# A recurrent attention, two expert layers and one core: the attention's small products laid out anew

## The chip, the cores and the metric

The program runs on one core of a Trainium2 chip, as one launch. The metric is device time in microseconds (us); lower is better. The engines are named as in the profile: PE (TensorE, matrix products), PEld (its weight loads), DVE (VectorE), ACT (ScalarE), POOL (GpSimd), SP (SyncE, which here only issues DMAs).

## The reference, cut to what matters

```python
def _attn_ref(r, k, v, w, a, b):          # batch 4, heads 8, 768 steps, head width 40
    state = np.zeros((B, H, D, D))
    for t in range(S):
        y[:, :, t] = np.einsum('bhd,bhde->bhe', rt, state)
        Sa = np.einsum('bhde,bhe->bhd', state, at)
        state_decay = state * wt[:, :, None, :] - np.einsum('bhd,bhe->bhde', Sa, bt)
        state = state_decay + np.einsum('bhd,bhe->bhde', vt, kt)
    return y

def reference(...):
    x = attention output as (3072 tokens, 320)
    x = moe(x)       # skip test, 8 experts, top 1: x + gate * relu(x @ w1[e]) @ w2[e], hidden 1024
    return ffn(x)    # h = x @ w_in (320 to 2048); (h * sigmoid(1.702 h)) @ w_out
```

Everything is fp32. The attention is a recurrence over 768 steps with a 40 by 40 state for each of 32 pairs of batch and head; the expert layer and the last layer are dense products over 3072 tokens.

## The kernel before, in words

**Attention.** The 768 steps are cut into 12 chunks of 64, and each chunk is solved with matrix products in fp32. Of the 128 partitions a half (64) belongs to one half of the batch (called hb, 0 or 1), and within a half there are two batch elements (par, 0 or 1) and 8 heads (h). One chunk does this:

- `g_load`, `g_prep`: the decays w are loaded and multiplied up by two scans on DVE (tile W; L212 and L225, with three small operations, L215 to L221, between them). One buffer `wt` holds the load, so the next chunk's w is loaded only when the scan has read it.
- `g_a`, `g_kb`: POOL scales a, k and b by W (tiles at, kbT). PE transposes k and b to km (L286), W to F (L247).
- `g_gram`, for a pair of chunks: PE forms the 32x32 diagonal blocks of the product of a and b (L312), ACT copies them to Za, DVE transposes them to Z (L322), and 62 DVE operations on tile tm (L336 and L339 in turn, 31 times) invert the unit triangular blocks. DVE transposes the result to Tc (L345), and DMAs put it in tz (L354), of which one chunk's chain reads.
- `g_ag` forms the full 64x64 product and masks it to tile m (L373, L378), `g_ab` forms the off-diagonal block again into tile bz (L401, L406).
- `g_chain`, once for each hb: X = m v + a S (L443, L450); then a block solve, x = -X, U = tz x, y = U, X += bz y, x = -X, U += tz x (L464 three times), with a copy on ACT between two products. tz and bz are 128 rows high, with zeros where the other batch element lies. The last U goes into vu.
- `g_state`: the next state from the old one and from k times vu (L508, L512), scaled on DVE (L516). `g_sn` transposes it (L536).
- `g_vt`, `g_pq`, `g_post`: transposes of vu (L558), products with r (L577), a mask on DVE (L579), and the output (L600, L605, L611).
- `put` and `logits` send the output to memory and form the expert logits (L837, L847); `g_route` assigns experts.
- `g_warm` puts products whose result nobody reads (L630) into PE's order.

An fp32 product is two records in the trace, an fp32 transpose one; a run of 32 products reads x64.

**Experts and last layer.** `Moe1` gathers the tokens of an expert, multiplies hi and lo fp16 parts (L1114, L1117), and again for the second product (L1153 to L1155). `Moe2` does the same with L1363, L1366 and L1403 to L1405. In L1117 and L1366 the third of three products has 64 rows of weights, the others 128.

**Order.** Nothing is a loop on the chip. Each step is a generator that yields what it waits for and what it will cost on which engine; `weave` runs through all generators and issues next what can start soonest by those costs, with the table RANK to break near ties. What comes out is one fixed order of instructions for each engine. PE, DVE, ACT, POOL and SP's DMA issue each work through their order, and wait in it.

## Time and profile before

| | |
|---|---|
| median of 3 runs | 1093.49 us (1087.88 to 1104.85) |
| profiled execution, its own time | 1083.23 us |
| profiled execution, span from first to last instruction | 1081.4 us |
| mean granted TensorE clock | 0.912 of full speed |
| PE busy | 954.4 us, 88% of the span |
| DVE, ACT, POOL busy | 588.2, 392.9, 373.1 us |

The span is read in stages: to about 117 us no chain has begun; from 117 to 536 us the chunks run; then the routing of the last tokens and the first gather; from 570 us the experts; from 727 us the last layer. [...]

### The profile page before, as it was taken

Reading aid. Unit: us, or ns where it says so; the run is one execution under the profiler, and the core shown is the slowest. Engines: PE = TensorE matmul, PEld = TensorE weight load, DVE = VectorE, ACT = ScalarE, POOL = GpSimd, SP = SyncE. Lnnn points to the kernel's source line nnn. Section 1 sums busy time; section 2 is a strip of 40 time slices with the busy share of each in tenths; the row PEclk is TensorE's granted clock in tenths of the full one; section 3 lists DMA queues with packets and bytes.
Section 4 is the critical chain, followed back from the end, with each engine's and each line's share of the span. In section 5 each row is a group of like instructions: output and inputs, shape, how many; then the busy total and the mean of one; then the engine's idle time right before and its main releaser. Section 6 shows DMA issues by size and latency. Waiting matters only on the chain.

```text
span 1081.4 us, 30855 instructions
## 1 busy us (share of the span) xinstructions
PE 954.4 (88%) x13709; PEld 706.2 (65%) x13709; DVE 588.2 (54%) x1070; ACT 392.9 (36%) x780; POOL 373.1 (34%) x277
## 2 busy tenths in 40 slices
PE   4677799999999999999607997959899999999998
PEld 4577689889888898989605774633455545555555
DVE  3589872795784954544998774579921121212110
ACT  0121234434334334234444653425433243333330
POOL 4673021333434321222234444325433243233320
PEclk8798599999999998699558997979999999999999
DMA  4332223434333232031688654442201010100000
GB/s 139 100 94 54 54 84 88 127 104 111 79 99 98 82 104 61 18 101 57 217 220 251 167 148 145 151 99 84 64 13 38 19 31 13 31 20 7 19 13 27
DMA packets 81586, 92.77 MB, mean 86 GB/s; under 512 B 58516, under 2 KB 68504, under 8 KB 77464
## 3 DMA queue, kind: packets, MB, share of 16 engines
q1 hardware_dynamic: 79144, 86.38, 28.0%
q0 software_dynamic: 2304, 4.36, 1.6%
q8 instruction: 109, 1.79, 0.7%
q14 instruction: 29, 0.24, 0.1%
HBM read 66.04 MB, written 14.48 MB: 74 GB/s over the span
## 4 chain that ended last, share of the span: by engine, by line
PE 59%; DVE 15%; DMA 10%; issue 7%; POOL 5%; ACT 2%; SPq 1%; POOLq 0%; DVEq 0%; ACTq 0%
PE g L1363 5%; PE c L1403 5%; PE c L1404 5%; PE c L1405 5%; PE g L464 4%; PE g L577 4%; PE g L1366 4%; DMA wt<-wt 3%; DMA w2s<-w 3%; PE gx L1363 3%; PE gx L464 2%; PE g L600 2%; PE g L605 2%; PE gx L443 2%; PE gx L450 2%
## 5 line engine op out<-in xcount | busy, mean ns | idle before, releaser
L1386 POOL TENSOR_TENSOR glo<-g,ghi 128x512 f16<-128x512 f32 x96 | 115.1, 1199 | 216.0 <-ACT ghi L1385 215.9
L1382 DVE SCALAR_TENSOR_TENSOR g<-g,sg 128x512 f32<-128x512 f32 x64 | 44.1, 690 | 144.8 <-ACT sg L1380 144.8
L1403 PE MATMUL c<-wo_hi,ghi 128*128 128x320 f16 x384 | 115.8, 302 | 2.6 <-ACT wo_hi L1308 2.6
L1404 PE MATMUL c<-wo_lo,ghi 128*128 128x320 f16 x384 | 115.1, 300 | 0.9 <-DVE wo_lo L1311 0.9
L1405 PE MATMUL c<-wo_hi,glo 128*128 128x320 f16 x384 | 115.2, 300 | 0.0
L1363 PE MATMUL g<-xt,wi_hi 128*128 128x512 f16 x320 | 81.8, 387 | 12.2 <-DMA xt<-xe 12.2
L1385 ACT CAST ghi<-g 128x512 f16<-128x512 f32 x96 | 59.3, 617 | 85.1 <-DVE g L1382 85.1
L1363 PEld LDWEIGHTS <-wi_hi 128*128 128x128 f16 x480 | 45.6, 99 | 59.0 <-DMA xt<-xe 12.5
L275 POOL TENSOR_TENSOR kbT<-kbT,W 128x1024 f32<-128x1024 f32 x24 | 64.3, 2689 | 40.7 <-DMA kbT<-kbT 22.5
L336 DVE TENSOR_TENSOR tmp<-tm,Z 128x252 f32<-128x252 f32 (+22 forms) x186 | 64.5, 347 | 10.3 <-PE tm L328 5.6
L1366 PEld LDWEIGHTS <-wi_lo 128*128 128x128 f16 (+1 forms) x288 | 27.9, 97 | 64.4 <-issue 42.2
L339 DVE TENSOR_TENSOR tm<-tm,tmp 128x252 f32<-128x252 f32 (+22 forms) x186 | 66.1, 355 | 5.1
L1380 ACT ACTIVATE sg<-g 128x512 f32<-128x512 f32 x64 | 38.0, 595 | 71.2 <-PE g L1366 71.2
L1382 DVE SCALAR_TENSOR_TENSOR g<-gx,sg 128x512 f32<-128x512 f32 x32 | 22.1, 689 | 76.3 <-ACT sg L1380 76.3
L464 PE MATMUL g<-x,tz 128*64 128x40 f32 x1536 | 58.2, 243 | 1.5 <-issue 1.3
L1366 PE MATMUL g<-xt,wi_lo 128*128 128x512 f16 (+1 forms) x192 | 59.2, 385 | 0.0
L1049 POOL TENSOR_TENSOR w2l<-w2s,w2h 128x1280 f16<-128x1280 f32 x16 | 42.7, 2671 | 47.5 <-ACT w2h L1047 46.6
L917 POOL DMA_INDIRECT tab<-c_pair,r_si x24 | 27.8, 1158 | 89.9 <-DVE c_pair L914 51.8
L464 PEld LDWEIGHTS g<-x,tz 128*64 128x64 f32 x1536 | 54.5, 153 | 4.2 <-issue 2.6
L261 POOL TENSOR_TENSOR at<-at,W 128x1024 f32<-128x1024 f32 x12 | 37.2, 3097 | 57.1 <-DMA at<-at 56.8
L1403 PEld LDWEIGHTS <-ghi 128*128 128x128 f16 x384 | 37.5, 98 | 28.4 <-issue 16.1
L630 PE MATMUL gx<-c 128*128 128x192 f16 x506 | 52.5, 258 | 3.8 <-DMA c<-c 3.7
(169 smaller groups left out, 2088.1 us busy)
## 6 DMA issues: line engine op xcount, KB each, us to landing
w2s<-w SPq DMA_DIRECT2D x8, 1280.0 KB
w1s<-w1a SPq DMA_DIRECT2D x8, 1024.0 KB
wt<-wt SPq DMA_DIRECT2D x24, 320.0 KB
vu<-rv SPq DMA_DIRECT2D x12, 640.0 KB
kbT<-kbT SPq DMA_DIRECT2D x24, 320.0 KB
d_s<-wo SPq DMA_DIRECT2D x10, 512.0 KB
d_s<-wia SPq DMA_DIRECT2D x8, 512.0 KB
rT<-rT SPq DMA_DIRECT2D x24, 160.0 KB
```

The costliest lines, as they stand in the source:

```text
L275: nc.gpsimd.tensor_tensor(out=t, in0=t, in1=w, op=ALU.mult)
L336: nc.vector.tensor_tensor(out=tv, in0=Tm[:, :, r0:, st:st + 1].to_broadcast([128, 2, n, st]), in1=Z4[:, :, st:st + 1, 0:st].to_broadcast([ ...
L339: nc.vector.tensor_tensor(out=Tm[:, :, r0:, 0:st], in0=Tm[:, :, r0:, 0:st], in1=tv, op=ALU.subtract)
L464: mm(z[o, d], lhsT=w[:, par, hb * 8 + h], rhs=t[:, h], start=start and h == 0, stop=True, **kw)
L1363: nc.tensor.matmul(h, lhsT=self.whi[:, k % 3, fs], rhs=xt[:, k], start=k == 0, stop=False)
L1366: nc.tensor.matmul(h, lhsT=self.wlo[:p, k, fs], rhs=xt[:p, k], start=False, stop=k == 2)
L1382: nc.vector.scalar_tensor_tensor(out=g, in0=h, scalar=2.0 ** -6, in1=sg2, op0=ALU.mult, op1=ALU.mult)
L1385: nc.scalar.copy(out=ghi[:, f], in_=g)
L1386: nc.gpsimd.tensor_tensor(out=glo[:, f], in0=g, in1=ghi[:, f], op=ALU.subtract)
L1403: nc.tensor.matmul(o, lhsT=ghi[:, f, s], rhs=self.ohi[:, f], start=f == 0, stop=False)
L1404: nc.tensor.matmul(o, lhsT=ghi[:, f, s], rhs=self.olo[:, f], start=False, stop=False)
L1405: nc.tensor.matmul(o, lhsT=glo[:, f, s], rhs=self.ohi[:, f], start=False, stop=f == 15)
```

## The change

- `g_chain` does both halves of the batch at once. Every product of X, U and the state has 64 rows and 64 columns of weights, in one of four places of the array: rows of one half, columns of one half, with the places changing from product to product. Moved columns are 48 or 64 where they were 40 (paddings are zeroed or not read).
- `g_ab` and bz are gone: `g_ag` is called for each par and forms, with a mask of two kinds (c_two), both the block that v needs and the off-diagonal block.
- `g_vt` transposes only the part of vu that is U, in halves of 64 rows; v's part comes from memory with rT. `g_pq` is 64 products of 40 rows and 64 columns in four places (uT and rT) in place of 16 of 80 rows and 128 columns. `g_post` has its second product (L582) in four places too.
- `g_gram`: the blocks of both chunks of a pair and of both batch elements lie on 128 partitions (tm is 32 by 32 on each), so Z and Tc are one transpose for a pair instead of two; the number of DVE operations stays at 62.
- `g_burst` adds 18 products that nobody reads to each of two places of each chunk, `g_warm` issues three of 128 columns where it issued two of 192, by another rule.
- Experts and last layer: the 64-row product is made a 128-row one (weights doubled). For it w1b is loaded twice from memory, and one more DMA copies lo weights of the last layer; a copy of w1h by DMA is gone.
- `weave` counts costs otherwise, many costs are other numbers, and RANK is another table, so that the order of all engines is another.

The diff, cut to its core:

```diff
--- before.py
+++ after.py
...
+                yield 'A.37'
+                nc.scalar.copy(out=Za[:, i, hb], in_=Ad[hb][:, :256])
+                self.give(sg[hb])
+        yield ('elim', c0 - 2)
+        Z = self.tile([128, 32, 32], F32, 'Z')
+        yield 'D1.95'
+        nc.vector.transpose(out=Z.rearrange('p t s -> p (t s)'), in_=Za.rearrange('p i b (g t) -> p t (i b g)', t=32))
...
         for st in range(31, 0, -1):
-            r0 = st // 2
-            n = 16 - r0
-            tv = tmp[:, :2 * n * st].rearrange('p (q a b) -> p q a b', q=2, b=st)
-            d = f'D{.06 + 2 * n * st / 960}'
+            n = 32 - st
+            tv = tmp[:, :n * st].rearrange('p (a b) -> p a b', b=st)
+            d = f'D{.17 + .00107 * n * st}'
             yield d
-            nc.vector.tensor_tensor(out=tv, in0=Tm[:, :, r0:, st:st + 1].to_broadcast([128, 2, n, st]),
-                                    in1=Z4[:, :, st:st + 1, 0:st].to_broadcast([128, 2, n, st]), op=ALU.mult)
+            nc.vector.tensor_tensor(out=tv, in0=Tm[:, st:, st:st + 1].to_broadcast([128, n, st]),
+                                    in1=Z[:, st:st + 1, 0:st].to_broadcast([128, n, st]), op=ALU.mult)
             yield d
-            nc.vector.tensor_tensor(out=Tm[:, :, r0:, 0:st], in0=Tm[:, :, r0:, 0:st], in1=tv, op=ALU.subtract)
+            nc.vector.tensor_tensor(out=Tm[:, st:, 0:st], in0=Tm[:, st:, 0:st], in1=tv, op=ALU.subtract)
         self.mark('elim', c0)
         yield ('te', c0 - 3)
         Tc = self.tile([128, 2, 512], F32, 'Tc', 2)
-        for i in range(2):
-            yield 'D1.0'
-            nc.vector.transpose(out=Tc[:, i].rearrange('p (g t d) -> p t d g', t=16, d=2), in_=Tm[:, i].rearrange('p a b -> p (a b)'))
+        yield 'D1.95'
+        nc.vector.transpose(out=Tc.rearrange('p i (u r) -> p r (i u)', r=32), in_=Tm.rearrange('p a b -> p (a b)'))
...
-                nc.sync.dma_start(out=tz[sl, 1 - q // 2, :, q % 2 * 32:q % 2 * 32 + 32], in_=Tc[sl, i].rearrange('p (u t) -> p u t', t=32))
+                nc.sync.dma_start(out=tz[sl, :, q % 2 * 32:q % 2 * 32 + 32], in_=Tc[sl, i].rearrange('p (u t) -> p u t', t=32))
...
-    def g_ag(self, c):
+    def g_ag(self, c, par):
...
         for h in range(8):
-            for par in range(2):
-                R = slice(64 * par, 64 * par + 64)
+            for q in range(2):
                 for hb in range(2):
                     r = slice(64 * hb, 64 * hb + 64)
-                    nc.tensor.matmul(ps[hb][R, 64 * h:64 * h + 64], lhsT=kbT[r, h, par, R], rhs=at[r, h, par], start=True, stop=True)
-        self.mark('ag', c)
+                    o = slice(64 * (q ^ hb), 64 * (q ^ hb) + 64)
+                    nc.tensor.matmul(ps[hb][o, 64 * h:64 * h + 64], lhsT=kbT[r, h, par, o], rhs=at[r, h, par], start=True, stop=True)
+        self.once('ag', c)
...
-    def g_ab(self, c):
...
-            for h in range(8):
-                for par in range(2):
-                    o = 64 - 64 * par
-                    nc.tensor.matmul(ps[o:o + 32, 32 * h:32 * h + 32], lhsT=kbT[r, h, par, o:o + 32], rhs=at[r, h, par, 32:],
-                                     start=True, stop=True)
...
+        self.once('gram', c)
...
-    def g_chain(self, c, hb):
-
-        nc = self.nc
-        yield (f'gram{hb}', c)
+    def g_chain(self, c):
...
+        every = [(h, par, hb, slice(48 * h, 48 * h + 48), slice(64 * par, 64 * par + 64), slice(64 * hb, 64 * hb + 64), slice(64 - 64 * hb, 128 - 64 * hb))
+                 for h in range(8) for par in range(2) for hb in range(2)]
+        yield 'P1.05*.40'
+        X = [self.pst(f'gx{hb}') for hb in range(2)]
+        self.X = X[1]
+        for h, par, hb, d, o, v, u in every:
+            mm(X[hb][o, d], lhsT=m[par][v, hb, h], rhs=vu[v, 16 * hb + 8 * par + h, :48], start=h == 0, stop=False, **kw)
...
+        for h, par, hb, d, o, v, u in every:
+            mm(X[hb][o, d], lhsT=at[v, h, par], rhs=ST[v, 8 * par + h, :48], start=False, stop=True, **kw)
...
-        times(U, self.tz, x)
-        self.once('U', c)
-        vu5 = vu.rearrange('p (b q h) x -> p b q h x', b=2, q=2)
+        x, y = self.x, self.y
+        x4, y4 = (z[:, :640].rearrange('p (b h d) -> p b h d', b=2, d=40) for z in (x, y))
+        v3 = lambda z, w: z[:, :8 * w].rearrange('p (h d) -> p h d', d=w)[:, :, :40]
+        for i in range(2):
+            for hb in range(2):
+                yield 'A.44'
+                nc.scalar.activation(out=x4[:, hb], in_=v3(X[hb], 48), func=AF.Copy, scale=-1.0)
+            if i:
+                self.mark('D', c)
+            yield '+g2'
+            sg = self.got
+            yield 'P1.05*.54'
+            U = [self.pst(z) for z in sg]
+            for h, par, hb, d, o, v, u in every:
+                mm(U[par][u, 64 * h:64 * h + 64], lhsT=tz[o, 8 * hb + h], rhs=x[o, 320 * hb + 40 * h:320 * hb + 40 * h + 64], start=h == 0, stop=True, **kw)
+            if i:
+                break
+            for par in range(2):
+                yield 'A.44'
+                nc.scalar.copy(out=y4[:, par], in_=v3(U[par], 64))
+                self.give(sg[par])
+            yield 'P1.05*.40'
+            for h, par, hb, d, o, v, u in every:
+                mm(X[hb][o, d], lhsT=m[par][u, hb, h], rhs=y[u, 320 * par + 40 * h:320 * par + 40 * h + 48], start=False, stop=True, **kw)
+            self.mark('B', c)
+        self.mark('U', c)
         for par in range(2):
-            R = slice(64 - 64 * par, 128 - 64 * par)
-            yield 'A.33'
-            nc.scalar.copy(out=vu5[R, hb, par], in_=v3(U)[R])
-        self.give(sc)
-        self.once('vu', c)
+            for hb in range(2):
+                yield 'A.42'
+                u = slice(64 - 64 * hb, 128 - 64 * hb)
+                o = 16 * hb + 8 * par
+                nc.scalar.copy(out=vu[u, o:o + 8, :40], in_=v3(U[par], 64)[u])
+            self.give(sg[par])
+        self.mark('vu', c)
...
-                    mm(ps[64 * hb:64 * hb + 40, 40 * h:40 * h + 40], lhsT=km[:, p], rhs=vu[:, p], start=False, stop=True, **kw)
+                    mm(ps[64 * hb:64 * hb + 40, 64 * h:64 * h + 64], lhsT=km[:, p], rhs=vu[:, p], start=False, stop=True, **kw)
...
-            ps = self.pst(sg)[:80]
-            for j in range(4):
-                o = 320 * q + 80 * j
-                nc.tensor.transpose(out=ps[:, 128 * j:128 * j + 128], in_=vu[:, o:o + 80], identity=self.C['c_id'])
...
+        for i in range(8):
+            for hb in range(2):
+                u = slice(64 - 64 * hb, 128 - 64 * hb)
+                nc.tensor.transpose(out=ps[hb][:, 64 * i:64 * i + 64], in_=vu[u, 16 * hb + 2 * i:16 * hb + 2 * i + 2].rearrange('p a b -> p (a b)'), identity=self.C['c_id'][u, u])
+        for hb in range(2):
...
-        for j in range(4):
-            i = hb * 8 + par * 4 + j
-            nc.tensor.matmul(ps[:, 128 * j:128 * j + 128].rearrange('p (e t) -> p e t', e=2), lhsT=vt[:, i], rhs=rT[:, :, i], start=True, stop=True)
...
+        for i in range(8):
+            for w in range(2):
+                for e in range(2):
+                    r = slice(64 * e, 64 * e + 40)
+                    o = slice(64 * (w ^ hb), 64 * (w ^ hb) + 64)
+                    src = uT[r, 8 * hb + i] if w else rT[r, 1, 8 * hb + i]
+                    nc.tensor.matmul(ps[e][o, 64 * i:64 * i + 64], lhsT=src, rhs=rT[r, 0, 8 * hb + i], start=True, stop=True)
+        pq = s[f'pq{hb}'] = self.tile([128, 8, 2, 64], F32, f'pq{hb}')
+        for e in range(2):
+            yield 'D.69'
+            nc.vector.tensor_tensor(out=pq[:, :, e], in0=ps[e].rearrange('p (i t) -> p i t', t=64),
+                                    in1=self.C['c_mask'].unsqueeze(1).to_broadcast([128, 8, 64]), op=ALU.mult)
...
+        yield 'P1.95*.91'
+        Y = [self.pst(z) for z in sg]
+        every = [(hb, j, par, e, slice(64 * par, 64 * par + 64), slice(256 * hb + 64 * j, 256 * hb + 64 * j + 64))
+                 for hb in range(2) for j in range(4) for e in range(2) for par in range(2)]
+        for hb, j, par, e, o, d in every:
+            mm(Y[e][o, d], lhsT=s[f'pq{hb}'][:, 4 * par + j, e], rhs=km[:, 640 * hb + 320 * par + 80 * j + 40 * e:640 * hb + 320 * par + 80 * j + 40 * e + 64], start=hb + j == 0, stop=False, **kw)
+        yield 'P1.05*.54'
+        for hb, j, par, e, o, d in every:
+            r = slice(64 * e, 64 * e + 40)
+            mm(Y[e][o, d], lhsT=rT[r, 0, 8 * hb + 4 * par + j], rhs=S[r, 4 * par + j, 64 * hb:64 * hb + 64], start=False, stop=True, **kw)
...
+    PACE, SURPLUS = .6, .1
+
+    def warm(self, n):
+        for i in range(n):
+            self.nc.tensor.matmul(self.X[:, 384:], lhsT=self.C['c_i'], rhs=self.C['c_tm'][:, :128],
+                                  start=self.first, stop=True, skip_group_check=True)
+            self.first = False
+
+    def g_burst(self, c, q):
+        yield ('warm', 0)
+        yield ('D', c - 1)
+        yield 'P1.0*1.08'
+        self.warm(18)
+        self.mark(f'b{q}', c)
...
             if owed > 0.0:
-                yield 'P.18*.38'
-                for i in range(2):
-                    self.nc.tensor.matmul(self.X[:, 320:], lhsT=self.C['c_i'], rhs=self.C['c_tm'][:, :192],
-                                          start=first, stop=True, skip_group_check=True)
-                    first = False
+                yield 'P.17*.18'
+                self.warm(3)
...
-            gens += [(d('ag'), self.g_ag(c)), (d('ab'), self.g_ab(c))]
-            for q in range(4):
-                gens += [(d('pq'), self.g_pq(c, q // 2, q % 2))]
+            gens += [(d('ag'), self.g_ag(c, 0)), (d('ag'), self.g_ag(c, 1)), (d('pq'), self.g_pq(c, 0)), (d('pq'), self.g_pq(c, 1))]
...
-        s1b = st.tile([128, 1024], F32, name='w1t')[:64]
-        yield 'Q.6>E.8'
-        nc.sync.dma_start(out=s1b, in_=self.pick('w1b', e))
+        s1b = st.tile([128, 1024], F32, name='w1t')
+        for q in (0, 64):
+            yield 'Q.6>E.8'
+            nc.sync.dma_start(out=s1b[q:q + 64], in_=self.pick('w1b', e))
...
-        yield 'A.9'
-        nc.scalar.activation(out=h1[:64, 2], in_=s1b, func=AF.Copy, scale=16.0)
-        yield 'Q.6>E.4'
-        nc.sync.dma_start(out=h1[64:, 2], in_=h1[:64, 2])
+        yield 'A1.05'
+        nc.scalar.activation(out=h1[:, 2], in_=s1b, func=AF.Copy, scale=16.0)
...
                 for k in range(3):
-                    n = 128 if k < 2 else 64
-                    mm(d, lhsT=l1[:n, k, fs], rhs=xt[:n, k], start=False, stop=k == 2)
+                    mm(d, lhsT=l1[:, k, fs], rhs=xt[:, k], start=False, stop=k == 2)
...
             nc.sync.dma_start(out=h[:64, 2, w], in_=h[64:, 2, w])
+            nc.sync.dma_start(out=l[64:, 2, u], in_=l[:64, 2, u])
             nc.sync.dma_start(out=l[:64, 2, w], in_=l[64:, 2, w])
...
             for k in range(3):
-                p = 128 if k < 2 else 64
-                nc.tensor.matmul(h, lhsT=self.wlo[:p, k, fs], rhs=xt[:p, k], start=False, stop=k == 2)
+                nc.tensor.matmul(h, lhsT=self.wlo[:, k, fs], rhs=xt[:, k], start=False, stop=k == 2)
...
                 yield ('U', NCH - 1)
+                yield ('b0', NCH - 1)
+                yield ('b1', NCH - 1)
                 yield ('Y', NCH - 3)
```

What it moves on the engines is seen at three places. The first is PE where the first chains run, before: g and gx are PSUM tiles, tz and bz the block inverses, x, y, m and vu as above.

```order
L464 MATMUL g_1418<-x_1410,tz 64x40 x16
L464 MATMUL g_1435<-x_1416,tz 64x40 x16
L464 MATMUL gx_538<-y_1452,bz_111 64x40 x16
L464 MATMUL gx_557<-y_1470,bz_111 64x40 x16
L464 MATMUL g_1418<-x_1493,tz 64x40 x16
L464 MATMUL g_1435<-x_1514,tz 64x40 x16
L443 MATMUL gx_1539<-vu,m_832 64x40 x16
L443 MATMUL gx_1566<-vu,m_824 64x40 x16
L508 MATMUL g_1585<-ST,c_86 128x320
L512 MATMUL g_1585<-vu,km 40x40 x16
```

Two chains, one for each hb, stand beside each other in runs of 16. The same place after, at the end of the step with y (L453); L601 are the products that nobody reads, L378 is `g_ag`.

```order
L453 MATMUL gx_831<-y,m_783 64x48
L453 MATMUL gx_832<-y,m_783 64x48
L453 MATMUL gx_831<-y,m_730 64x48
L453 MATMUL gx_832<-y,m_730 64x48
L601 LDWEIGHTS c_88
L601 MATMUL gx_832<-c_88 128x128
L601 LDWEIGHTS c_88
L601 MATMUL gx_832<-c_88 128x128
L601 LDWEIGHTS c_88
L601 MATMUL gx_832<-c_88 128x128
L378 MATMUL g_1740<-at_98,kbT_99 64x64
```

Both halves of the batch now stand in one run of 32, product by product in turn, and between the steps stand other products and L601.

The second place is DVE in the first inversion, before: L336 and L339 are the inversion, the others the decays of a later chunk.

```order
L339 TENSOR_TENSOR tm<-tm,tmp 128x2x4x24
L212 SCALAR_TENSOR_TENSOR W<-wt,c_d_90 128x1024
L336 TENSOR_TENSOR tmp<-tm,Z 128x230
L215 TENSOR_TENSOR tots<-W,wt 128x32
L339 TENSOR_TENSOR tm<-tm,tmp 128x2x5x23
L219 RECIPROCAL tot<-tots 128x32
L336 TENSOR_TENSOR tmp<-tm,Z 128x220
L221 COPY c_d_93<-tot 128x16
L339 TENSOR_TENSOR tm<-tm,tmp 128x2x5x22
L336 TENSOR_TENSOR tmp<-tm,Z 128x252
L339 TENSOR_TENSOR tm<-tm,tmp 128x2x6x21
L225 SCALAR_TENSOR_TENSOR W<-wt,c_d_93 128x1024
```

Two chunks' decays stand within it (this one and one more behind it). After, at its beginning, and then at its end:

```order
L229 SCALAR_TENSOR_TENSOR W<-wt,c_d_93 128x1024
L330 STREAM_TRANSPOSE Z<-Za 128x1024
L383 TENSOR_TENSOR m_1037<-g_1003,c_86 128x512
L383 TENSOR_TENSOR m_1037<-g_1004,c_86 128x512
L343 TENSOR_TENSOR tmp<-tm,Z 128x31
L346 TENSOR_TENSOR tm<-tm,tmp 128x31
L343 TENSOR_TENSOR tmp<-tm,Z 128x60
```

```order
L346 TENSOR_TENSOR tm<-tm,tmp 128x30x2
L343 TENSOR_TENSOR tmp<-tm,Z 128x31
L346 TENSOR_TENSOR tm<-tm,tmp 128x31
L216 SCALAR_TENSOR_TENSOR W<-wt,c_d_90 128x1024
L351 STREAM_TRANSPOSE Tc<-tm 128x32x32
L219 TENSOR_TENSOR tots<-W,wt 128x32
```

Between these two pieces stand only the rest of the inversion and two more masks (L383); of the decays one scan stands ahead of Tc.

## Rows read from the trace of the kernel before

**Rows 1.** Stretches: us, busy us (instructions) of each engine, granted clock, DMA share, GB/s.

```profile
0.00:117.00 117.00, 74.19 (x1472) 66.90 (x1472) 80.56 (x111) 15.61 (x38) 60.58 (x34) 0.81 0.34 93
117.00:536.00 419.00, 404.24 (x9419) 367.32 (x9419) 263.09 (x574) 164.70 (x407) 120.35 (x99) 0.92 0.33 91
...
570.00:727.00 157.00, 128.96 (x898) 91.73 (x899) 111.72 (x188) 71.38 (x96) 65.98 (x42) 0.89 0.55 158
727.00:1081.40 354.40, 346.61 (x1920) 180.19 (x1918) 102.13 (x145) 126.89 (x223) 115.11 (x96) 0.99 0.11 31
```

**Rows 2.** Timeline of PE, 213 to 228 us: start, length, line, tiles, weights, columns.

```profile
213.22 2.06 PE L464 MATMUL g<-x,tz 128*64 128x40 f32 x64
215.10 2.04 PE L464 MATMUL gx<-y,bz 128*64 128x40 f32 x64
...
220.81 1.16 PE L577 MATMUL g<-rT,vt 80*128 80x128 f32 x8
221.81 0.60 PE L286 MATMUL g<-c,kbT 128*128 128x128 f32 x4
222.34 0.70 PE L401 MATMUL g<-at,kbT 64*32 64x32 f32 x32
222.97 1.16 PE L373 MATMUL g<-at,kbT 64*64 64x64 f32 x64
224.06 0.70 PE L401 MATMUL g<-at,kbT 64*32 64x32 f32 x32
...
225.68 0.82 PE L630 MATMUL gx<-c 128*128 128x192 f16 x8
226.34 0.60 PE L558 MATMUL g<-c,vu 128*80 128x128 f32 x4
226.87 1.16 PE L600 MATMUL g<-km,pq 128*64 128x40 f32 x32
```

**Rows 3.** Timeline of PE, 206 to 210 us.

```profile
206.43 0.81 PE L512 MATMUL g<-vu,km 128*40 128x40 f32 x32
207.07 1.11 PE L605 MATMUL g<-S,rT 80*64 80x40 f32 x32
208.10 0.76 PE L312 MATMUL g<-at,kbT 64*32 64x32 f32 x64
208.79 1.13 PE L450 MATMUL gx<-ST,at 64*64 64x40 f32 x32
209.85 0.55 PE L837 MATMUL g<-c,xo 128*128 128x128 f32 x3
```

**Rows 4.** A stretch within the chunks, columns as in the first group.

```profile
424.00:451.00 27.00, 25.68 (x446) 23.96 (x445) 12.86 (x41) 6.19 (x15) 3.90 (x5) 0.51 0.02 7
```

**Rows 5.** The chain that ended last, first run of the first chain: start, us.

```profile
117.14 3.57 PE g L464 x64
```

**Rows 6.** DVE groups, 66 to 112 us: busy, mean ns, idle before.

```profile
L225 DVE TENSOR_TENSOR_SCAN W<-wt,c_d 128x1024 f32<-128x1024 f32 x2 | 5.7, 2860 | 0.0
L212 DVE TENSOR_TENSOR_SCAN W<-wt,c_d 128x1024 f32<-128x1024 f32 x2 | 5.0, 2516 | 1.7 <-DMA wt<-wt 1.7
L215 DVE TENSOR_TENSOR tots<-W,wt 128x32 f32<-128x32 f32 x2 | 4.0, 1983 | 0.0
```

**Rows 7.** Timeline of DVE: the transposes ahead of and behind the first inversion.

```profile
65.91 1.95 DVE L322 STREAM_TRANSPOSE Z<-Za 128x1024 f32<-128x1024 f32 x1
...
111.14 1.04 DVE L345 STREAM_TRANSPOSE Tc<-tm 128x512 f32<-128x512 f32 x1
```

**Rows 8.** Timeline of PE in the last layer, from 1002.8 us.

```profile
1002.82 1.24 PE L1363 MATMUL g<-xt,wi_hi 128*128 128x512 f16 x5
1003.90 0.91 PE L1366 MATMUL g<-xt,wi_lo 128*128 128x512 f16 x3
1004.75 0.31 PE L1403 MATMUL c<-wo_hi,ghi 128*128 128x320 f16 x1
```

**Rows 9.** The chain that ended last, a piece among the experts.

```profile
651.22 7.48 DMA w2s<-w
```

464 lines of the change are left out of this document (197 added, 267 removed), and 48 rows, old and new, of the table RANK.

## The prediction, made before the changed kernel ran

> **What bounds the kernel now.** I read the table of stretches first [rows 1]. From 117 to 536 us PE is busy 404 of 419 us, DVE 263, ACT 165: the chunks are bound by PE. In the last layer it is PE again (347 of 354). Among the experts PE has 129 of 157 us and no engine fills the stretch. Until 117 us PE waits for the first inversion: the first run of a chain starts at 117.14 [rows 5], just behind the transpose that ends the inversion on DVE [rows 7]. So three questions decide: what the PE work of the chunks weighs, when the first chain starts, and at what granted clock PE works. The clock was 0.92 of full speed in the chunks and 0.51 in one stretch of them in which PE was listed busy [rows 1, 4], so this is not for free.
>
> **Prices.** In [rows 2, 3] a run's cost is the step from its start to the next one's: L464 of 32 products 215.10 − 213.22 = 1.88 us; L577 of four 1.00; L401 of 16 0.63; L373 of 32 1.09; L558 of four 0.53; L630 with eight records of 192 columns 0.66, or 0.0825 each; L605 of 16 1.03; L312 of 32 0.69; L450 of 16 1.06; L512 of 16 0.64. A record (an fp32 product is two) costs 29 ns in L464 and 33 in L450, but only 17 in L373, whose products go to four places of the array in turn, by halves of rows and of columns. The change puts nearly all small products into that form, so L373 is the row that I price them by.
>
> **Chunks: the PE queue.** I count products in both orders from the first tz product to the end of the attention; kinds whose number and form stay cancel. What goes or changes:
>
> - L464: 1,152 products, 36 runs × 1.88 = 67.7. L443: 352, the same form, × 1.88 = 20.7. L450: 22 runs × 1.06 = 23.3.
> - L577: 48 × 1.00 = 48.0. L605: 24 × 1.03 = 24.7. L558: 48 × 0.53 = 25.4.
> - L373: 9 × 1.09 = 9.8. L401: 20 × 0.63 = 12.6. L312: 16 × 0.69 = 11.0. Fillers L630: 78 × 0.0825 = 6.4.
>
> Together 249.6 us. What stands there after:
>
> - products in four places (L378, L422, L427, L444, L453, L554, L582): 3,648, or 114 runs × 1.09 = 124.3;
> - L530, 192 smaller transposes: 48 runs of four × 0.2 = 9.6, an estimate between L373's price (6.4 in all) and L558's (25.4);
> - L320: 18 × 0.69 = 12.4;
> - products that nobody reads (L601), 1,272 of 128 columns: by columns 0.055 each, 70.0. Before, 78 stand there, so this takes back over half of what the rest saves.
>
> Together 216.3: 33 us less. Two groups of products move 64 columns in place of 40 (L483 and L578). L512 costs 0.64 and L605 1.03 with 40 moved columns each; what differs is the columns of weights (40 and 64), so I take moved columns nearly free: 4 us more, bounds 0 and 24 (in proportion to columns). **Queue: −29.** Besides, L444 and L582 (1,152 products) change their half of the rows only at every second product; L450, which never changes it, costs 33 ns per record and L373 17, so they can cost up to 18 us more; none is taken, since the halves of columns do change from product to product, and the 18 stay in the range.
>
> [...]
>
> **Chunks: the start.** Between the transposes Z and Tc [rows 7] DVE spends 65.9 to 111.1 us on the inversion and on two later chunks' decays: scans L225 5.7 and L212 5.0, L215 4.0, a wait of 1.7 for a load [rows 6], and the small operations between them. In the new order one scan (2.5) stands there, and Tc is one transpose of twice the size (+0.9); the 62 operations stay, at about the same size. That frees 5.7 + 5.0 + 4.0 + 1.7 − 2.5 − 0.9 = 13, with the small operations about 15. The decays come later, when DVE has room (263 busy of 419, and some 15 more are within PE's shadow). **Start: −15**, so the first chain at about 102 us; bounds −5 (the other masks and loads now ahead of it fill the gap) and −20. The loads of w move with the decays on SP's queue; I price them at nothing, since DMAs are used to 0.34 there [rows 1], and at 2 us (the 1.7 above) if a scan then waits for its load with chains behind it. ACT (165 of 419) has room for its copies, which are of other shapes now.
>
> **Chunks: clock and idling.** Before, PE is idle 419 − 404 = 15 us. [...] After: one chain in place of two means that each hand-over from PE to ACT and back shows unless other products stand between, and the order has g_ag, pq, post or L601 there. I take 25 us idle and 11 lost by the clock in the last chunk, where little stands between: **−10**, bounds −35 and +15. The attention together: −15 − 29 − 10 = −54.
>
> **Experts.** The 64-row product becomes 128-row. In the last layer [rows 8] a run of five products of 512 columns takes 1.08 (0.216 each), and the three of which one has 64 rows 0.85, where three by that price take 0.65: the odd one costs 0.20. Here products are half as wide and 64 groups save at most 12.8; but the chain there runs mostly through loads of weights, such as w2s with 7.48 us [rows 9], and w1b is now loaded twice. I take **−3**, bounds −10 and +13 (the bytes that come on top, 2.1 MB, at the 158 GB/s of this stretch [rows 1]).
>
> **Last layer.** 96 groups × 0.20 = 19; PE is bound there at clock 0.99 [rows 1, 8] but for the first block: **−17**, bounds −12 and −19. The extra copy of lo weights is a DMA in a stretch that uses 11% of them, so nothing.
>
> Sum: −54 − 3 − 17 = −74. Span 1081.4 − 74 = 1007.4; outside it the profiled execution has 1083.23 − 1081.4 = 1.8, so 1009. The median of the runs stands 10.3 above that execution, and I carry that: **1019 us**. The bounds are not all met at one time; as a range of this case I take 985 to 1052.
>
> **Rivals.**
>
> - *Small products don't overlap (slower).* If products in four places cost like L450, 33 ns a record, 7,296 records × 16 ns = 117 us more: 1136. From 27 ns a record (74 / 7,296 = 10 more) on, the gain is gone. For it: L450 is a 64-row product as well, and the chain's products write rows by turns of another kind than L373. Against it: L373 itself, with the same weights and columns, 17 ns in many runs. Chance 0.06. [...]
> - *The clock falls.* If L601 does not hold it, since it stands elsewhere than the waits, and another 80 us pass at the lower level, 1 − 1.88 / 3.57 = 0.47 of them is lost [rows 2, 5], 38 us: 1057. For it: in 424 to 451 us the clock was 0.51 while PE was listed busy 25.7 of 27 [rows 4]. Against it: 16 times as many fillers. From 74 / 0.47 = 157 us more at the lower level on, the change would bring nothing. Chance 0.10.
> - *One chain's hand-overs.* Five times in a chunk PE needs ACT's copy of what it has just made. If each shows 1.2 us in 12 chunks, 72 us are idle in place of 25: 1066; or PE waits for the inversions on DVE (263 + 15 us of work in a stretch of 380) with a like result, 1055 to 1090. For it: before, two chains covered each other. Against it: the work that stands between. Chance 0.13.
>
> **How the numbers follow.** The forecast has 0.68, the rivals 0.06, 0.10 and 0.13, and 0.03 is left for something slower that I don't see. Within 2% (1071.6 to 1115.4, about what a measurement of this kernel tells from no change) lie the upper half of the third rival, and the tail of the second: 0.09. Slower holds the first, and what is left: 0.08. Faster: 0.83. The range of 8 in 10 reaches from 978 (start and clock both at their good bound) to 1085, which takes in the clock's case and most of the hand-overs'.
>
> **What would show it.** In the trace after: the first L444 run starts at about 102 us; a warm run of 32 products of L444, L453 or L554 steps by about 1.1 us (2.1 is the first rival); the attention's last products end some 54 us before 536; three L1354 products step by 0.65, not 0.85; PE's idle time in the chunks is about 25 us, and the granted clock 0.95 or more. What would make the prediction wrong is a run of L444 that steps differently from L378 though both use four places, or idle time at the copies of x and y.

## The result and the profile after

The changed kernel takes 1057.26 us (median of 4; 1047.44 to 1059.06) where the kernel before takes 1095.11 (median of 4): ratio 0.966, 95% interval 0.957 to 0.975. It is faster, by about half of the forecast (1019 us), and its time lies inside the range on record (978 to 1085) but above the forecast's own (985 to 1052). The profiled execution has a span of 1054.3 us against 1081.4. Ratios here compare undisturbed executions alone, medians are of all.

The table of stretches after, columns as in [rows 1], with the gap ahead of the experts apart:

```profile
0.00:114.00 114.00, 79.36 (x1651) 75.55 (x1651) 60.40 (x100) 12.27 (x29) 47.32 (x38) 0.85 0.39 93
114.00:538.00 424.00, 375.58 (x11944) 336.58 (x11942) 269.48 (x582) 124.92 (x331) 124.20 (x101) 0.93 0.36 96
538.00:576.00 38.00, 5.45 (x23) 4.06 (x24) 27.66 (x57) 20.70 (x29) 17.27 (x10) 0.50 0.63 196
576.00:715.00 139.00, 112.78 (x898) 95.56 (x897) 107.88 (x190) 71.85 (x96) 69.04 (x40) 0.92 0.66 191
715.00:1054.30 339.30, 326.59 (x1920) 188.58 (x1918) 110.44 (x152) 127.44 (x224) 114.76 (x96) 0.99 0.12 34
```

Put beside [rows 1], this says at once where the gain did not come from. The chunks take no less than before (424 us beside 419), with PE listed as busy 376 us in place of 404, 29 us less, and with 33 us more idle time. The clock is nearly the same (0.92 and 0.93). The gain is in the two last stages. Measured again (a_again below), the ratio is 0.980 (0.972 to 0.989), so that the gain comes out as 3.4% once and as 2.0% once.

By the first and last instructions of each stage (first tz product, last transpose of the logits, first expert product, first product of the last layer):

| stage, profiled execution | before | after | change | forecast |
|---|---|---|---|---|
| start to the first chain | 117.1 | 114.2 | −3 | −15 |
| chunks, to the last logits | 414.8 | 427.7 | +13 | −39 |
| to the first expert product | 38.6 | 33.6 | −5 | 0 |
| experts | 156.3 | 139.1 | −17 | −3 |
| last layer | 354.6 | 339.7 | −15 | −17 |

The prices of the small products came out as read. PE's timeline in the chunks after:

```profile
190.00 1.16 PE L444 MATMUL g<-x,tz 64*64 64x64 f32 x64
191.10 0.66 PE L251 MATMUL g<-c,W 128*128 128x128 f32 x4
...
192.45 1.21 PE L453 MATMUL gx<-y,m 64*64 64x48 f32 x64
193.59 0.66 PE L292 MATMUL g<-c,kbT 128*128 128x128 f32 x4
...
203.61 1.09 PE L487 MATMUL g<-vu,km 128*40 128x64 f32 x32
204.64 0.84 PE L601 MATMUL gx<-c 128*128 128x128 f16 x12
```

L444 steps by 1.10 us for 32 products and L453 by 1.14 (17 and 18 ns per record), where L464 took 1.88 [rows 2]. L487 with 64 moved columns steps by 1.03, where L512 with 40 took 0.64 [rows 3]. Yet what these runs save does not arrive. PE's waits in the chunks after (what waited, for what: us in total, times, longest):

```profile
PE g L320 <- issue: 13.3, 8, 3.5
PE g L827 <- DVE xo L590: 9.5, 1, 9.5
PE gx L427 <- issue: 5.7, 3, 2.7
PE gx L601 <- issue: 4.2, 4, 2.0
PE g L578 <- issue: 3.6, 2, 2.7
PE g L444 <- issue: 2.7, 3, 1.1
PE gx L601 <- ACT x L436: 2.5, 5, 0.6
```

ACT and DVE, the third rival's suspects, hardly stand there but for one wait of 9.5 us at the end. The large item is "issue": PE waits for nothing that the profile shows, 34 us in all (6 before). Here is one such wait, in the middle of a run of products that depend on nothing new:

```profile
168.59 1.14 PE L320 MATMUL g<-at,kbT 64*32 64x32 f32 x110
173.23 0.42 PE L320 MATMUL g<-at,kbT 64*32 64x32 f32 x18 [3.49 <-issue]
```

and a line from the profile's list of DMA queues (packets, MB, share), which holds more than one would read into it:

```profile
q8 instruction: 131, 2.15, 0.9%
```

131 packets of 16 KB are PE's program itself: 32,983 instructions of PE stand in the trace (weight loads, products and its sequencer's), 252 to a packet. The DMA records say when each packet started and landed. Of PE's idle stretches of over 0.2 us in the chunks 28, with 35 us in all, end 1.2 to 1.6 us after a packet has landed, and from one of the 28 to the next PE goes through a multiple of 256 instructions, to within one, in 26 of 27 cases. The 7 such waits of before (6 us) stand at the same distances. The other idle stretches after are short ones, most of them ahead of L601, and the wait of L827. In the chunks there are 93 packets after and 74 before, and none starts closer than 3.3 us behind the one ahead of it. A run in four places issues 128 instructions in 1.1 us, so that it uses up a packet in 2.2.

### The profile page after: what moved, and what is told of

Same layout as the page of the kernel before. It is cut to its first block, busy times and chain, and to the rows that moved or that the text cites. A ratio compares the mean times of both kernels' runs of the same rounds, so it can differ in the third digit from the quotient of the medians.

```text
span 1054.3 us, 36252 instructions
## 1 busy us (share of the span) xinstructions
PE 899.8 (85%) x16428; PEld 700.3 (66%) x16428; DVE 575.9 (55%) x1080; ACT 357.2 (34%) x708; POOL 372.6 (35%) x283
## 4 chain that ended last, share of the span: by engine, by line
PE 61%; DVE 13%; issue 11%; DMA 7%; ACT 3%; POOL 2%; SPq 2%; DVEq 0%; ACTq 0%; POOLq 0%
PE gx L601 8%; PE g L1352 5%; PE c L1392 5%; PE c L1393 5%; PE c L1391 5%; PE g L1354 3%; PE g L578 3%; PE g L444 3%; PE gx L1352 2%; PE g L554 2%; PE g L378 2%; PE g L487 2%; PE g L292 2%; PE g L483 1%; DMA kbT<-kbT 1%
## 5 line engine op out<-in xcount | busy, mean ns | idle before, releaser
L601 PE MATMUL gx<-c 128*128 128x128 f16 x2073 | 147.6, 227 | 11.8 <-issue 4.5
L601 PEld LDWEIGHTS <-c 128*128 128x128 f16 x2073 | 130.7, 102 | 19.1 <-issue 9.4
L805 POOL TENSOR_TENSOR xr<-xo,xr 128x256 f16<-128x256 f32 (+1 forms) x44 | 21.2, 502 | 169.4 <-ACT xr L801 169.3
L279 POOL TENSOR_TENSOR kbT<-kbT,W 128x1024 f32<-128x1024 f32 x24 | 60.8, 2553 | 40.3 <-DMA kbT<-kbT 37.8
L343 DVE TENSOR_TENSOR tmp<-tm,Z 128x31 f32<-128x31 f32 (+15 forms) x186 | 63.3, 340 | 9.9 <-PE tm L336 4.1
L346 DVE TENSOR_TENSOR tm<-tm,tmp 128x31 f32<-128x31 f32 (+15 forms) x186 | 64.8, 349 | 5.9
L383 DVE TENSOR_TENSOR m<-g,c 128x512 f32<-128x512 f32 x48 | 31.1, 681 | 51.7 <-PE g L378 51.7
L1103 PE MATMUL g<-g_xt,w1h 128*128 128x240 f16 x220 | 31.5, 275 | 25.5 <-DMA g_xt<-g_x 25.4
L1354 PE MATMUL g<-xt,wi_lo 128*128 128x512 f16 x192 | 53.1, 386 | 0.0
L1354 PEld LDWEIGHTS <-wi_lo 128*128 128x128 f16 x288 | 28.5, 99 | 34.9 <-issue 1.6
```

Of the source, the lines that this page charges most:

```text
L279: nc.gpsimd.tensor_tensor(out=t, in0=t, in1=w, op=ALU.mult)
L343: nc.vector.tensor_tensor(out=tv, in0=Tm[:, st:, st:st + 1].to_broadcast([128, n, st]), in1=Z[:, st:st + 1, 0:st].to_broadcast([128, n, st ...
L346: nc.vector.tensor_tensor(out=Tm[:, st:, 0:st], in0=Tm[:, st:, 0:st], in1=tv, op=ALU.subtract)
L601: self.nc.tensor.matmul(self.X[:, 384:], lhsT=self.C['c_i'], rhs=self.C['c_tm'][:, :128], start=self.first, stop=True, skip_group_check=True)
L1354: nc.tensor.matmul(h, lhsT=self.wlo[:, k, fs], rhs=xt[:, k], start=False, stop=k == 2)
```

## The theories

*Supply*: runs in four places use up instructions faster than packets of 256 come in; the gaps behind packets eat what the cheaper products save. *Rivals*: the gaps have another cause (the products' own conflicts, data transfers); fillers are what PE waits through, in hand-overs to ACT that were there anyway; the clock takes everything back. For the experts: *order* (loads of weights start earlier) against *rows* (the 128-row product).

In the table below are the runs' chunks, each from its own profile. "Work" is the number of PE records of each kind times their step in undisturbed runs of the profile after (of before for the first two rows), "behind packets" PE's idle time that ends 1.0 to 1.8 us after an instruction packet landed, "other idle" the rest of its idle stretches of over 0.2 us, "rest" what is left: records at the lower clock (0.50 of full speed, the only level under 1.00 in the traces before and after), and what the joins between runs cost beyond these prices.

| kernel | chunks us | work | behind packets | other idle | rest | clock | packets |
|---|---|---|---|---|---|---|---|
| before | 414.8 | 355 | 6 | 6 | 48 | 0.92 | 74 |
| b_wide | 430.8 | 355 | 5 | 9 | 62 | 0.89 | 74 |
| after | 427.7 | 346 | 35 | 14 | 33 | 0.93 | 93 |
| a_again | 428.3 | 346 | 33 | 15 | 35 | 0.93 | 93 |
| a_narrow | 424.2 | 346 | 39 | 13 | 27 | 0.94 | 93 |
| a_fill64 | 447.5 | 349 | 55 | 10 | 34 | 0.95 | 104 |
| a_nofill | 413.8 | 275 | 49 | 32 | 58 | 0.89 | 84 |
| a_nofill2 | 419.0 | 275 | 53 | 31 | 59 | 0.89 | 84 |
| a_nopace | 423.8 | 298 | 47 | 27 | 52 | 0.89 | 87 |
| a_noburst | 437.5 | 324 | 55 | 15 | 45 | 0.90 | 90 |
| a_few | 401.6 | 336 | 28 | 12 | 26 | 0.95 | 79 |
| a_nofill_few | 385.2 | 265 | 36 | 31 | 53 | 0.89 | 69 |

b_wide has the attention of before, a_again and a_narrow that of after, in the same order: one profile of the same chunks differs from another by up to 16 us before, 4 after, mostly with the clock. So the change is worth between −7 and +13 us in the chunks: nothing, where −39 was forecast.

How "rest" divides can be counted. For each kind of product take the mean time from one record's start to the next in its own profile at granted clock 1.00, idle stretches of over 0.2 us left out, and price all its records in the chunks by it. Then work with its joins is 376 us before and 357 after (377 in b_wide, 359 in a_again), records at the lower clock cost 27 and 22 us beyond that, and 12 and 49 us are idle. So the work fell by 19 us rather than by the table's 9, and the clock gave back 5. "Behind packets" can be checked as well: in every kernel of the table nearly all these waits stand at one place of PE's program: 193 or 194 instructions beyond a multiple of 256, as the trace counts them. By place they come to 34.5 us after, 33.0 in a_again, 27.1 in a_few, 47 in a_nofill and in a_nofill2 and 30.0 in a_nofill_few; in the last two 6 us of the table's figure stand elsewhere, at waits for ACT or DVE that end behind a packet by chance.

## The experiments

### m_rate: the rate of instructions by itself

A program of its own with the four stretches named in the expectation; its core:

```diff
+for i in range(96):
+    for j in range(8):
+        q, b = j // 2 % 2, j % 2
+        mm(ps[b][h(q ^ b), :48], lhsT=wf[h(b), 64 * j:64 * j + 64], rhs=xf[h(b), :48], start=True, stop=True)
```

> A program of its own: no attention, no experts, no last layer; its output is a constant. On PE it has four stretches with fillers (128 columns) between them: (1) 768 fp32 products of 64 rows and 64 columns of weights in four places of the array in turn, 48 moved columns, with no other traffic; (2) the same while 10 MB of weights are loaded; (3) 768 products that all use the same half of the rows, 40 moved columns; (4) 24 runs of 32 products in four places with 18 fillers behind each. Theory 'supply': PE's instructions come in packets of 256 (16 KB), at best some 3.5 us apart, so that (1) starts at 17 ns per record and falls to about 27 once the instructions in hand are used up: 36 to 42 us for 1,536 records, with gaps that end 1.2 to 1.5 us after a packet has landed; (2) the same or somewhat longer; (3) 29 to 33 ns per record without gaps, 45 to 50 us; (4) 164 instructions in 2.1 us, just at the limit: 50 to 56 us. Rival 'the gaps in the changed kernel have another cause': (1) and (2) 1,536 x 17 ns = 26 us, and no gaps.

The first stretch in PE's timeline:

```profile
32.13 3.69 PE L1476 MATMUL ps<-xf,wf 64*64 64x48 f32 x235
36.94 2.08 PE L1476 MATMUL ps<-xf,wf 64*64 64x48 f32 x128 [1.12 <-issue]
40.40 2.08 PE L1476 MATMUL ps<-xf,wf 64*64 64x48 f32 x128 [1.38 <-issue]
44.12 2.08 PE L1476 MATMUL ps<-xf,wf 64*64 64x48 f32 x128 [1.65 <-issue]
47.58 2.08 PE L1476 MATMUL ps<-xf,wf 64*64 64x48 f32 x128 [1.38 <-issue]
```

235 records (470 instructions) run on at once, 14.9 ns from start to start, then exactly 128 records (256 instructions) between two waits of 1.1 to 1.7 us each, although no data move and no engine but PE works. The four stretches in the windows (PE, PEld, DVE, POOL, clock, DMA share, GB/s):

```profile
32.00:73.50 41.50, 24.98 (x1540) 23.55 (x1537) 0.00 (x0) 0.00 (x0) 1.00 0.02 4
83.80:138.50 54.70, 31.36 (x1538) 29.79 (x1536) 0.00 (x0) 0.00 (x0) 0.81 0.47 193
155.40:234.10 78.70, 78.70 (x1538) 78.66 (x1536) 0.00 (x0) 0.00 (x0) 0.53 0.01 2
252.80:307.80 55.00, 53.22 (x1952) 48.81 (x1950) 0.00 (x0) 0.00 (x0) 1.00 0.02 4
```

1,536 records take 41.3 us, 26.9 ns each over all, at full clock: supply, by its number. Packets there start 3.35 to 4.11 us apart. The DMA records show how these times come about: a packet starts 1.0 to 1.5 us after PE has gone on into the one before it (38.08 behind 36.94 us, say), is under way for 0.9 to 1.4, and PE goes on 1.2 to 1.5 after it has landed, some 3.6 us in all, while the packet in hand is worth 1.9 us of PE's time. The fillers ahead of the stretch use up a packet in some 7.1 us, which leaves time to fetch more, and yet no more than the 470 instructions were in hand: time won where instructions were few did little where they were many. While weights are loaded, the first packets are 6.1 to 7.1 us apart and the waits 2.8 to 4.5 us; this stretch was also partly at the lower clock (0.81 in the mean). The third has a clock of 0.53 and takes 51 ns per record; the 29 to 33 ns expected of it were meant for the full clock, and no run shows them there. The fourth, runs of 32 products with 18 fillers behind each, is just at the limit: 55.0 us with waits of 0.2 to 0.7. The rival (26 us and no gaps) is out. It is one execution of one program.

### b_wide and a_narrow: the 128-row product alone, and the change without it

```diff
 b_wide, in both stages:
-p = 128 if k < 2 else 64
-nc.tensor.matmul(h, lhsT=self.wlo[:p, k, fs], rhs=xt[:p, k], start=False, stop=k == 2)
+nc.tensor.matmul(h, lhsT=self.wlo[:, k, fs], rhs=xt[:, k], start=False, stop=k == 2)
 a_narrow: the same lines the other way round
```

> The kernel before with one part of the change alone: the third lo product with 128 rows in the experts and in the last layer (with the loads and the copy that it takes). Theory 'order': the last layer gets 15 us shorter (96 x 0.2 less a part), the experts 0 to 5, so 1093 goes to about 1075; the 17 us that the changed kernel gains among the experts come from the new order of loads. Rival 'rows': the 128 rows bring the experts' 17 us too: about 1061.

> The changed kernel with the third lo product back at 64 rows in the experts and in the last layer, loads and copies left as they are; the order is the same. 'Order': the last layer gets 15 us longer, the experts 0 to 5: 1057 goes to about 1075. 'Rows': 32 us longer, about 1089.

b_wide: 1083.35 us beside 1093.23; before's executions beside it lie between 1071 and 1114 us, so that the whole times decide nothing and the stages are to be read: last layer 338.8 us (354.6 before), experts 156.3 (156.3). a_narrow: 1074.23 us; last layer 353.8 (339.7 after), experts 143.9 (139.1 to 141.4 in the two profiles of the changed kernel). So the product is worth 14 to 16 us in the last layer, 0 to 5 among the experts. At least 12 of the experts' 17 us come from the order: the chain there before has w2s loads of 7.5 us [rows 9], and after none of its five longest pieces is one. That the earlier loads as such are the gain was not tried by itself, so what in the order brings it stays open.

### a_fill64: more instructions, the same columns

```diff
-for i in range(n):
-    self.nc.tensor.matmul(self.X[:, 384:], lhsT=self.C['c_i'], rhs=self.C['c_tm'][:, :128],
+for i in range(2 * n):
+    self.nc.tensor.matmul(self.X[:, 384:448], lhsT=self.C['c_i'], rhs=self.C['c_tm'][:, :64],
```

> The changed kernel with every filler L601 as two of 64 columns in place of one of 128: the same columns, places and order, 2,544 PE instructions more in the chunks (10 packets). 'Supply': gaps of PE that end 1.2 to 1.5 us after an instruction packet lands grow from 33 us in the chunks to 45 to 60, and the time by 10 to 30 us. Rival 'it is not the number of instructions': gaps within 5 us of 33, time within 1%.

1077.77 us beside 1104.12, ratio 0.976 (0.968 to 0.985). Fillers cost 29 ns a record, 75 us in all in place of 72. 11 packets more, gaps behind packets 35 to 55 us, chunks 427.7 to 447.5, at a higher clock (0.95): gaps and chunks each 20 us longer, inside what supply expected. The whole time does not show it: beside the ratio of 0.976 stand 0.966 (0.957 to 0.975) and 0.980 (0.972 to 0.989) for the changed kernel.

### a_nofill, a_nofill2, a_nopace, a_noburst: the fillers

```diff
 def warm(self, n):
+    if ('D', 0) in self.done:
+        return
 a_nopace, a_noburst: the same test ahead of self.warm(3), or of self.warm(18), alone
```

> The changed kernel without the products that nobody reads (L601) once the first chunk's chain is through its second half; all else in the same order. Theory 'queue and supply': their 72 us stand in PE's queue, but without them runs in four places stand closer and wait for instructions more, and some clock is lost: chunks 424 us go to about 390, idle time of PE from 40 to 80 us: total about 1025. Rival 'hand-overs': the fillers only lie in waits for ACT that are there anyway: chunks unchanged within 8 us, PE idle 70 us longer, waiting for ACT by the profile. Rival 'clock': without them the granted clock falls below 0.8 in the chunks, and these get 30 us or more longer: about 1090.

> The changed kernel without the 840 paced fillers of the chunks (47 us by columns) once the first chain is through its second half; the 432 of the bursts stay. If the bursts are what holds the clock: clock in the chunks 0.91 or more, chunks 15 to 25 us shorter, total 1030 to 1040. If all fillers weigh alike: 10 us shorter at a clock of 0.90 to 0.91, 1047.

> The changed kernel without the bursts of 18 fillers (432, 24 us by columns) from the second chunk on; the paced ones stay. If the bursts hold the clock: clock in the chunks 0.90 or less, time unchanged or up to 10 us longer. If all fillers weigh alike: 5 us shorter, 1052.

> The changed kernel itself, unaltered, beside the next two on one chip. Its own spread: 0.966 of before, within its interval; chunks 424 to 430 us; the first chain between 104 and 114 us (profiles of kernels with the same start gave 104 to 116).

> The changed kernel without the fillers of the chunks once more, beside the changed kernel: if the fillers cost more than they give, 0.95 of before and 10 to 20 us less than the changed kernel; if the first run was a lucky one, within 5 us of it.

a_nofill: 1038.80 us beside 1093.23. a_nofill2, with the changed kernel (a_again) on the same chip: 1044.23 against 1058.32, ratios to before 0.962 (0.953 to 0.971) and 0.980 (0.972 to 0.989). So the kernel without the chunks' fillers beats both kernels. The 0.980 lies outside the interval that a_again was expected to keep to; its chunks (428.3 us) and its first chain (113.4) came out as expected. But of 72 us of work it keeps 9 to 14: the table has 14 to 18 us more behind packets (13 to 14 counted by place; dense runs stand closer together), 18 more of other idle time, 25 more in the rest, of which the lower clock is 10 (22 to 32). Each theory explains a part, none the whole; my 390 us for the chunks was wrong (414 and 419). a_nopace (1059.73 beside 1104.12, ratio 0.970, 0.952 to 0.988) and a_noburst (1057.78, 0.966, 0.949 to 0.984) do not differ from the changed kernel by more than their intervals. a_noburst came out as expected if the bursts hold the clock (0.90, chunks 10 us longer); a_nopace met neither of its expectations (clock 0.89, chunks 4 us shorter). Since the clock fell with the bursts left in too, the bursts by themselves are not what keeps it.

### a_cols40: moved columns

```diff
-mm(ps[64 * hb:64 * hb + 40, 64 * h:64 * h + 64], lhsT=km[:, p], rhs=vu[:, p], start=False, ...)
+mm(ps[64 * hb:64 * hb + 40, 64 * h:64 * h + 40], lhsT=km[:, p], rhs=vu[:, p, :40], start=False, ...)
 likewise 64 to 40 columns in L578 and L582
```

> The changed kernel with 40 moved columns in place of 64 in L487 (the state), L578 and L582 (the output); same products, same order. By the two traces L487 costs 32 ns per record with 64 columns where L512 cost 23 with 40, L578 38 where L600 cost 33. 'Moved columns cost': these fall back, 6.2 + 3.4 us, total 1047 to 1051. 'Moved columns are free' (the step of my prediction): nothing changes within 3 us.

L487 falls from 32.0 to 23.2 ns per record, 6.2 us in all, as expected; L578 steps by 31.5 ns with 64 columns and by 31.2 with 40 in runs without a wait, so its price is not one of columns. The time does not follow: 1062.02 us, ratio 0.974 (0.953 to 0.996), chunks 429.9 at a clock of 0.90 (0.93). Records at the lower clock cost 31 us there, by the count above, in place of 22, more than the columns saved. That this is no accident of one profile, the mean clocks of whole executions suggest: 0.910 to 0.918 in its four, 0.922 to 0.942 in the ten of the changed kernel. The term was mis-sized; on the whole it decides nothing.

### a_fill32: fewer instructions in the fillers

```diff
+        wide = ('D', 0) in self.done
+        self.owe = getattr(self, 'owe', 0.0) + n * 55.0
+        while self.owe >= 0.0:
+            self.nc.tensor.matmul(self.X[:, 384:], lhsT=self.C['c_id' if wide else 'c_i'],
+                                  rhs=self.C['c_id'] if wide else self.C['c_tm'][:, :128],
...
+            self.owe -= 295.0 if wide else 55.0
```

> The changed kernel with the chunks' fillers as fp32 products of 128 columns (one for each 295 ns of fp16 fillers owed): the same PE time by the price of 147 ns per fp32 record of 128 columns (from L483, 367 ns for 320), but some 960 instructions in place of 2,544. 'Supply': gaps behind instruction packets fall from 35 us to 20 to 30, since 2,544 instructions more made them 20 longer; chunks 5 to 15 us shorter, if such products hold the clock as well (0.93). Rival 'number of instructions does not matter': gaps and chunks unchanged. Rival 'clock': granted clock below 0.90 and no gain.

1053.31 us beside 1058.32 for a_again, ratio to before 0.973 (0.967 to 0.979). Packets fell from 93 to 87, but the gaps behind them did not (41 us), nor did the chunks (431 us, clock 0.92). The fillers came out 11 us cheaper than meant (61 us), so that the dense runs stood closer, which may have cost as much again. The expectation failed: thinning out the sparse stretches did nothing here for the dense ones, as the 470 instructions in hand in m_rate would have it.

### a_few and a_nofill_few: fewer instructions in the dense runs

Shortened to the products themselves:

```diff
-nc.tensor.matmul(ps[e][o, 64 * i:64 * i + 64], lhsT=src, rhs=rT[r, 0, 8 * hb + i], start=True, stop=True)   # 32 of them
+nc.tensor.matmul(ps[e][:, 128 * i:128 * i + 128], lhsT=self.C['c_i'], rhs=self.C['c_tm'][:, :128], ...)      # 8, and
+nc.tensor.matmul(ps[e][:, :128], lhsT=uT[r, 8 * hb:8 * hb + 2], rhs=rT[r, 0, 8 * hb:8 * hb + 2], ...)        # 2
-mm(Y[e][o, d], lhsT=rT[r, 0, 8 * hb + 4 * par + j], rhs=S[r, 4 * par + j, 64 * hb:64 * hb + 64], ...)        # 32
+mm(Y[e][:, 128 * i:128 * i + 128], lhsT=rT[r, 0, 2 * i:2 * i + 2], rhs=S[r, i], ...)                         # 4
```

> The changed kernel with two groups of its small products put in fewer, larger ones of about the same PE time: L554 (32 products in four places, 128 instructions, 1.09 us) by eight fp16 products of 128 columns and two fp32 ones of 128 (24 instructions, about 0.95 us), L582 (128 instructions, 1.05 us) by four fp32 products of 128 columns (16 instructions, about 1 us). Neither part of the output is computed, so only the stage of the chunks is to be read (tokens go to other experts). 3,840 PE instructions fewer in the chunks, 15 of 93 packets, at PE time unchanged within 5 us. 'Supply': PE's gaps behind instruction packets fall from 33 to 39 us to 10 to 20, and the chunks from 428 us to 400 to 415. Rival 'the gaps belong to the other dense runs and only move': gaps 30 or more, chunks 420 to 430.

> The same in the kernel without the fillers of the chunks (again without that part of the output; the chunks alone are to be read). There the gaps behind packets were 49 to 53 us and the chunks 414 to 419. 'Supply takes back what the fillers cost': gaps 25 to 35, chunks 390 to 400. Rival 'clock and waits take it back': gaps may fall, but the granted clock (0.89) or the waits for ACT (31 us of idle time) rise, chunks 405 or more.

The chunks of a_few as a row of the windows:

```profile
106.90:508.60 401.70, 361.42 (x10033) 319.51 (x10032) 273.85 (x588) 129.06 (x338) 121.88 (x101) 0.95 0.38 101
```

14 packets fewer, chunks 427.7 to 401.6. By the table 10 of these 26 us are work (the products put in are cheaper than I meant), 7 the gaps behind packets (35 to 28; 10 to 20 were expected), 2 other idle, 7 the rest. Without fillers: 413.8 to 385.2, of which 10 are work, 13 the gaps (49 to 36; by place 47 to 30, inside the 25 to 35 expected), 5 the rest. So instructions in dense runs do cost time, but with the fillers in the gaps fell less than I had expected: those that stay sit mostly in L444, L320 and L378, which are as dense as before.

## Why the prediction was wrong, step by step

- **The queue, −29.** With every record at its kind's mean price at full clock the work fell by 19 (376 to 357); in the table's prices, without the joins between runs, by 9 (355 to 346). The price on which I staked most held: the runs in four places weigh 123 us, 124 in the prediction, and the first rival (33 ns per record) is out. The fillers weigh 72 (70), L530 8 (10), L320 11 (12). Too high were the prices of what goes: one row of each, with its neighbours, gave 250 us for what weighs 239 in the table's prices (L450 19.7, not 23.3; L577 43.5, not 48; L558 22.6, not 25.4). The wide columns cost 6.2, in L487 alone (4 taken).
- **Clock and idling, −10.** Here the largest step failed. It sets 36 us (25 idle, 11 lost by the clock) against 46 for the kernel before, 15 idle and 31 that I put down to the clock. No run shows the 31: the trace of before has the clock at 0.50 of full speed for 67 of the 419 us, and by the count above that cost 27 us, with 12 idle. I expected the idle time to grow by 10 us, to 25, at hand-overs, and a better clock (0.95 or more) to give back 20. The clock gave back 5 (27 to 22 us; 0.92 to 0.93), and 37 us of idle time came on top, 29 behind instruction packets and 8 elsewhere: +32 in place of −10. I priced L373's 17 ns from single runs of 64 records, 128 instructions each where m_rate had 470 in hand, and multiplied it by 114. That a price read from a short run may not hold for a long row of them, m_rate shows: 14.9 ns for the first 235 records, 26.9 over all. I had no term for the supply of instructions, which is to say that I put it at nothing, though the kernel before has such waits too (6 us). Why the clock gave back so little stays open. What I should have weighed, m_rate shows: 256 instructions between two waits, 470 in hand at the start, 214 more than one packet, and 3.35 to 4.1 us from packet to packet.
- **The start, −15.** −3 in this profile, −1 to −12 over the profiles of kernels with the same start (104.6 to 116.1). My DVE sum held: Z to Tc takes 32.0 us, 45.2 before. I took Z to begin at 65.9 as before. It does so only after the second chunk's L320, and on the way there PE waits for instructions, in L378 and in L320. In the profile after:

```profile
57.00 0.69 PE L378 MATMUL g<-at,kbT 64*64 64x64 f32 x10 [5.28 <-issue]
...
72.43 0.29 PE L320 MATMUL g<-at,kbT 64*32 64x32 f32 x14 [2.52 <-issue]
...
72.80 0.65 ACT L325 COPY Za<-g 128x256 f32<-128x256 f32 x2 [3.52 <-PE g L320]
...
73.47 2.00 DVE L330 STREAM_TRANSPOSE Z<-Za 128x1024 f32<-128x1024 f32 x1 [6.05 <-ACT Za L325]
```

  Z starts 7.6 us later, and these two waits are 7.8. In a_nopace, with the same order up to there, the same ten records of L378 wait 0.2:

```profile
51.59 0.44 PE L378 MATMUL g<-at,kbT 64*64 64x64 f32 x10 [0.23 <-issue]
```

  There Z starts at 65.7 and the first chain at 104.6, 2.6 us behind my 102. One packet decides it: it starts at 49.1 to 50.0 us in the four profiles whose chain begins by 106.9, and at 53.5 to 55.1 in the seven others, where L378 waits 4.7 to 5.6 us. So the start failed on the supply of instructions too; why the packet is late in some executions, these runs don't show. From Tc to the first chain it takes 8.7 us in place of 5.9, with fillers and transposes of W (L251) between.
- **Experts, −3:** −17, because of the new order (at least 12 by a_narrow), which I had not looked at there; that it is the loads in it was not tried. The product itself is worth what I took. **Last layer, −17:** −15, by the mechanism named; three products step by 0.64 us (850.49 to 851.13 below), not 0.85 [rows 8].

```profile
850.49 0.81 PE L1354 MATMUL g<-xt,wi_lo 128*128 128x512 f16 x3
851.13 0.30 PE L1391 MATMUL c<-wo_hi,ghi 128*128 128x320 f16 x1
```

- **The 10.3 us carried** from the profiled execution to the median stood for an odd execution of before; after, the median lies 1.1 above. That made up, by luck, 9 of the 47 us by which the terms were too good.
- **Rivals.** The clock did not fall further (0.92 before, 0.93 after), and waits for ACT did not come (one line with 2.5 us among the waits above). What they were to cost came through a mechanism that none of them named; that the second rival's number, 1057, is the time measured is an accident.

Open: how much of the chunks' time would come back if instructions were free. a_few and a_nofill_few bound it only from below (7 us for 14 of 93 packets, and 13 to 17 for 15 of 84). And why clock, waits and packets together give back four fifths or more of the fillers' time, I can only divide up, not explain.

## What to carry to other kernels

A change that makes products smaller and more is to be priced twice: by the step of a run, and by PE instructions in each dense stretch, since 256 of them took some 3.6 us to arrive in the steady row of m_rate, or 28 ns for each fp32 record with its weight load. Over the whole stage this sum would have warned of nothing: 93 packets at 3.6 us are 335 of the chunks' 428. It bound where more instructions than those in hand (470 in m_rate, some four runs in four places) followed one another faster than that. Waits marked "issue" inside runs that depend on nothing new, at distances of 256 instructions, were the sign. Products that are there only for the clock (0.93 with them in the chunks, 0.89 without) are work in PE's queue as well, 72 us here, and leaving them out is a cheap trial: here it was worth some 14 us.
